# Attention and feed-forward kernel: wide masks built on GpSimd, the first keys and weights loaded from ScalarE's queue, a new launch order, and four buffers for the last tile's stores

## The chip, the cores and the metric

The kernel runs on one NeuronCore of one Trainium2 chip. The metric is the device time of one execution in microseconds (us). Time before: 910.72 us, the median of three runs (909.49 to 911.6).

## The reference

Banded attention over 8 batches, 8 heads, 576 positions and 64 dimensions, and then a feed-forward block on the 4608 tokens of width 512:

```python
scores = scale * np.matmul(q, k.transpose(0, 1, 3, 2))
mask = (rel >= 0) & (rel < 64)                      # rel = query position - key position
scores = np.where(mask, scores, -1000000000.0)
attn = softmax(scores)
x = np.matmul(attn, v)                              # heads joined: 4608 x 512, float32
h = x @ w_in                                        # 512 -> 2048, float64 weights
g = np.where(h >= 1, h, np.where(h <= -1, 0.0, (h + 1) ** 2 / 4))
out = (g @ w_out).astype(np.float32)                # 2048 -> 512
```

## The kernel before

The tokens are cut into 9 tiles of 512 tokens. **Attention** goes in 36 steps of 128 tokens (two blocks of 64), four steps for a tile. A step s loads queries (`load_q`), keys (`load_k`) and two blocks of values (`load_v`); makes scores on TensorE in two halves h, the even and the odd heads (`att_scores`); takes the maximum on VectorE (`att_max`), the exponential on ScalarE (`att_exp`, four heads, eight records), the inverse of the sum and the product with it on VectorE (`att_inverse`, `att_normalize`), turns the result over (on TensorE with a copy out for the first seven steps, `att_transpose_pe` and `att_transposed`; on VectorE later), multiplies with the values (`att_values`), and splits the product into a high and a low part (`att_high`, `att_low`), the tiles `xh` and `xl`. For the first four steps the mask is added by TensorE, as a matmul of an identity `idr` with a rounded mask `mskr`; for the next three VectorE adds a wide mask of 128 columns; later steps use a narrow one of 96 columns.

**Weights** come as float64, one chunk f for 128 of the 2048 hidden units, unit 0 for `w_in` and unit 1 for `w_out` (512 KB each; from chunk 4 on both units in one load of 1 MB). ScalarE and VectorE convert the bits to a high and a low float part, in nine rows: `w_rest` and `w_sign` (ScalarE, out `u` and `raw`), two `w_limit` rows and `w_shift` (VectorE), `w_join` (VectorE), `w_high` (ScalarE), `w_low` (VectorE). **The feed-forward part** of tile t goes over the 16 chunks: `ffn_in` (12 matmuls into `ps_h`), the activation on ScalarE, VectorE and (from tile 1 on) GpSimd, and `ffn_out` (matmuls into `acc`). After the last chunk `ffn_take` copies `acc` into a tile `o` (two buffers) and `ffn_store` sends it out.

The order on each engine is not written by hand. Every piece of work is given to `Plan.add` with a key, a cost per engine, what it needs and what buffers it takes. `Plan.run` places the pieces by these numbers, and each engine's queue holds them in that order and runs them strictly one after the other. All loads and stores are issued from SyncE's queue (SP). At most eight transfers are under way before the next issue waits for an old one to land.

The masks, wide and narrow, come from memory by `load_masks` as the first transfer; `round_masks` then makes `idr` and `mskr` on ScalarE.

Of the kernel before, what the change touches and what calls it, by code (L numbers as in the profile page):

```python
# [44 lines left out]
W_LATE = 2.92
W_LOAD = 1580
V_LATE = 2.54
W0_KEY = -101.5
M_LATE = -3.29
W0_STEP = 2.63  # L50
FINE = 4
NWARM = 8
A_FIRST = (-100.64, -97.76, -95.51, -95)
A_NEXT = 3.31
A_STEP = 4.3
A_SPAN = 9
A_LEAD = 5
O_LAG = 2.5
DMA_LAG = 2300
BEGIN = dict(PE=1500, ACT=2300, DVE=2500, SP=750)  # L60
# [8 lines left out]
B_PE = 2050  # L69
B_DUE = 1.0, 2.5, 0.5  # L70
B_STEP = 16 / 3
B_FIRST = 3.5
A_END = 1.5
V_PE = 1270
NORM = dict(Pool=800, DVE=560), dict(DVE=690)
# [4 lines left out]
class Plan:  # L80
# [82 lines left out]
def banded_attention_then_ffn(ctx: ExitStack, tc: tile.TileContext, q, k, v, w, masks, out, dims):  # L163
# [25 lines left out]

    idt = const.tile([P, P], F32, name="idt")  # L190
    make_identity(nc, idt)
    msk = const.tile([P, 3, 2 * WIN], F32, name="msk")
    idr = const.tile([P, P], F32R, name="idr")
    mskr = const.tile([P, 3, WIN], F32R, name="mskr")
    wpool = ctx.enter_context(tc.tile_pool(name="wpool", bufs=1))

    ptd = [const.tile([P, NP, SB], F32, name=f"ptd{i}") for i in range(BUFS["ptd"])]
    for t in ptd:
# [118 lines left out]
    def variant(s):  # L317
        firsts = [(2 * s + i) % NB == 0 for i in range(2)]
        return 1 if firsts[0] else 2 if firsts[1] else 0

    def near(s):
        return s >= PE_STEPS

    def load_q(s):
        qts[s] = t = ld.tile([P, NP, SB], F32, name="qt", bufs=BUFS["qt"])
        nc.sync.dma_start(out=t, in_=q[s])

    def load_k(s):
# [34 lines left out]

    def att_masked(s, h):
        ps, sm, _, _ = blk[s, h]
        at, n = (WIN, NEAR) if near(s) else (0, WIN)
        m = msk[:, variant(s), at:at + n].unsqueeze(1).broadcast_to([P, NP, n])
# [73 lines left out]
    def add_step(t, i):  # L441

        s = starts[t] // SB + i
        masked = s < PE_MASKS
        joined = SOON <= s < NT // SB - 1
        pt, pv = ("ps_h", "acc") if s < LENT else ("ps_a", "ps_a")
        ps = "acc" if s < FIRST and s % 2 else "ps_a"
        if s < FIRST:
            key = due = A_FIRST[s]
        elif s >= SOON:  # L450
            key = a_keys[s]
        else:
            key = a_keys[s]
            due = min(key + A_SPAN, soon(s))
        lk = key - L_LEAD
        if s == 0:
            last["m"] = add(lk + M_LATE, dict(SP=590), lambda e: load_masks(), lag=DMA_LAG)
            last["r"] = add(lk + M_LATE, dict(ACT=480), lambda e: round_masks(), [last["m"]])
        xq = add(lk, dict(SP=790), lambda e: load_q(s), takes=["qt"], lag=DMA_LAG)
        xk = add(lk, dict(SP=1180), lambda e: load_k(s), takes=["kt"], lag=DMA_LAG)  # L460
        xv = add(lk + V_LATE, dict(SP=790), lambda e: load_v(s, 0), last["v"], takes=["vt"], lag=DMA_LAG)
        xw = add(lk + V_LATE, dict(SP=790), lambda e: load_v(s, 1), [xv], takes=["vt"], lag=DMA_LAG)
        last["v"] = [xw]
        needs = [xq, xk] + [last["r"]] * masked + last["s"]
        if s - 1 in before:
            needs_v, gives_v, split = before.pop(s - 1)

            def do(e):
                att_scores(s, masked, ps)
                att_values(s - 1, "ps_h")  # L470

            xs = add(
                key, dict(PE=B_PE), do, needs + needs_v, takes=[ps, ps, "sm", "sm", "ps_h"],
                gives=[("qt", xq), ("kt", xk)] + gives_v,
            )
            split(xs, key, "ps_h")
        else:
            xs = add(
                key, dict(PE=S_PE[near(s)] + 500 * masked), lambda e: att_scores(s, masked, ps), needs,
                takes=[ps, ps, "sm", "sm"], gives=[("qt", xq), ("kt", xk)],  # L480
            )
        last["s"] = [xs]
        ready, first, taken = [], last["t"], []
        for h in range(2):
            x = xs
            if s >= SOON:
                due = key + B_DUE[0] + B_DUE[2] * h
            if not masked:
                x = add(due, dict(DVE=MASKED[near(s)]), lambda e, h=h: att_masked(s, h), [x, last["m"]], gives=[(ps, xs, h)])
            x = add(due, dict(DVE=950 if masked else MAXIMUM[near(s)]), lambda e, h=h: att_max(s, h, masked), [x])  # L490
            x = add(
                due, dict(ACT=1750 if masked else EXP[near(s)]), lambda e, h=h: att_exp(s, h, masked), [x],
                gives=[(ps, xs, h)] * masked,
            )
# [24 lines left out]
        gives = [("ptd", taken[0]), ("ptd", taken[1]), ("vt", xv), ("vt", xw)]  # L519

        def split(xo, due, pv):
            after = [xo] if i == 0 else [xo, x_first[t]]
            x = add(due, XHIGH, lambda e: att_high(t, i, e), after, takes=["x"] if i == 0 else [])
            if i == 0:
                x_first[t] = x
            x = add(due, dict(DVE=660), lambda e: att_low(t, i), [x], gives=[(pv, xo)])
            x_ready.setdefault(t, []).append(x)

        if joined:
            before[s] = needs, gives, split  # L530
# [58 lines left out]

    os = {}  # L590

    def ffn_take(t, i, eng):
# [31 lines left out]
    def add_ffn(t):  # L624
        first, before, x_out = {}, [x_in[t - 1]] if t else [], {}
        for f in range(NF):
            for r, key in parts(t, f):
# [29 lines left out]
                for k, i in enumerate(subs(r)):  # L657
                    x_out[i] = xo
                    first.setdefault(i, (xo, k))
        for i in range(TILES[t] // P):  # L660
            xo = add(
                key, dict(DVE=690, ACT=590), lambda e, i=i: ffn_take(t, i, e), [x_out[i]], takes=["o"],
                gives=[("acc", *first[i])],
            )
            add(key, dict(SP=790), lambda e, i=i: ffn_store(t, i), [xo], lag=DMA_LAG, gives=[("o", xo)])


    a_keys, key = {}, float("inf")
# [77 lines left out]
```

## Time and profile before

| what | value |
|---|---|
| median of three runs | 910.72 us |
| the profiled execution | 909.63 us, of which its span from first to last instruction is 907.6 us |
| TensorE (PE) busy | 885.1 us, 98% of the span |
| VectorE (DVE) busy | 567.1 us, 62% |
| ScalarE (ACT) busy | 453.9 us, 50% |
| GpSimd (POOL) busy | 168.6 us, 19% |
| mean granted TensorE clock | 0.995 |

Busy time is the time in which an engine had an instruction running; for PE the ends are modelled, so a busy PE is not always at its peak. The shares are means over stages that differ: the first 55 us, in which nothing can be multiplied before it is loaded and converted, the long stretch after that, and the last 5 us.

### The profile page before, as it was taken

Reading aid. Unit: us, or ns where it says so; the run is one execution under the profiler, and the core shown is the slowest. Engines: PE = TensorE matmul, PEld = TensorE weight load, DVE = VectorE, ACT = ScalarE, POOL = GpSimd, SP = SyncE. Lnnn points to the kernel's source line nnn. Section 1 sums busy time; section 2 is a strip of 40 time slices with the busy share of each in tenths; the row PEclk is TensorE's granted clock in tenths of the full one; section 3 lists DMA queues with packets and bytes.
Section 4 is the critical chain, followed back from the end, with each engine's and each line's share of the span. In section 5 each row is a group of like instructions: output and inputs, shape, how many; then the busy total and the mean of one; then the engine's idle time right before and its main releaser. Section 6 shows DMA issues by size and latency. Waiting matters only on the chain.

```text
span 907.6 us, 17441 instructions
## 1 busy us (share of the span) xinstructions
PE 885.1 (98%) x6888; PEld 729.6 (80%) x6888; DVE 567.1 (62%) x1406; ACT 453.9 (50%) x1148; POOL 168.6 (19%) x142
## 2 busy tenths in 40 slices
PE   6789999999999999999999999999999999999997
PEld 5678788888888888888888888888888888888886
DVE  5999987778766666666666666667666766622111
ACT  6898965544544445444544443445444444433333
POOL 0000001212222221222122222122212221222221
PEclk8999999999999999999999999999999999999999
DMA  8982023111221122111211121112111220001001
GB/s 314 380 353 70 21 85 115 55 60 53 77 76 54 53 77 76 53 54 53 100 53 54 48 77 43 42 51 99 53 54 53 77 76 25 12 1 47 1 0 47
DMA packets 29281, 70.14 MB, mean 77 GB/s; under 512 B 3216, under 2 KB 3600, under 8 KB 29200
## 3 DMA queue, kind: packets, MB, share of 16 engines
q1 hardware_dynamic: 29200, 69.03, 21.8%
q8 instruction: 54, 0.88, 0.4%
q14 instruction: 27, 0.22, 0.1%
HBM read 59.58 MB, written 9.44 MB: 76 GB/s over the span
## 4 chain that ended last, share of the span: by engine, by line
PE 89%; DVE 6%; ACT 2%; issue 1%; DMA 1%; SPq 0%; ACTq 0%; DVEq 0%
PE acc L585 41%; PE ps_h L544 40%; PE ps_h L420 3%; PE ps_a L356 3%; DVE u L271 1%; ACT wts L215 1%; DVE raw L248 1%; DVE wts L283 1%; DMA raw<-in_w 1%; PE ps_a L420 1%; DVE gl L576 1%; DVE raw L260 1%; DVE sm L391 1%; PE ps_a L406 0%; ACT u L267 0%
## 5 line engine op out<-in xcount | busy, mean ns | idle before, releaser
L544 PE MATMUL ps_h<-xh,wts 128*128 128x512 f32 (+1 forms) x1232 | 382.5, 376 | 3.5 <-DVE a L566 2.9
L585 PE MATMUL acc<-wts,gh 128*128 128x512 f32 x1152 | 360.2, 394 | 0.0
L576 POOL TENSOR_TENSOR gl<-a,gh 128x512 fp32r<-128x512 f32 (+1 forms) x135 | 167.1, 1238 | 730.4 <-ACT gh L571 724.8
L544 PEld LDWEIGHTS ps_h<-xh,wts 128*128 128x128 f32 x1232 | 227.0, 188 | 47.2 <-DVE a L566 3.5
L566 DVE SCALAR_TENSOR_TENSOR a<-a,ps_h 128x512 f32<-128x512 f32 (+1 forms) x154 | 100.2, 652 | 256.0 <-ACT a L559 240.4
L585 PEld LDWEIGHTS acc<-wts,gh 128*128 128x128 f32 x1152 | 212.9, 188 | 45.0 <-issue 0.3
L544 PE MATMUL ps_h<-xl,wts 128*128 128x512 f32 (+1 forms) x616 | 231.4, 376 | 0.6 <-DVE xl L433 0.6
L585 PE MATMUL acc<-wts,gl 128*128 128x512 f32 x576 | 224.3, 389 | 0.0
L554 ACT ACTIVATE a<-ps_h 128x512 f32<-128x512 f32 (+1 forms) x154 | 87.8, 570 | 262.4 <-PE ps_h L544 260.5
L400 DVE STREAM_TRANSPOSE ptd<-sm 32x128 f32<-32x128 f32 x696 | 210.7, 303 | 10.9
L571 ACT CAST gh<-a 128x512 fp32r<-128x512 f32 (+1 forms) x154 | 91.0, 592 | 102.5 <-DVE a L566 88.6
L544 PEld LDWEIGHTS ps_h<-xl,wts 128*128 128x128 f32 x616 | 115.9, 188 | 21.8 <-DVE xl L433 0.8
L585 PEld LDWEIGHTS acc<-wts,gl 128*128 128x128 f32 x576 | 108.1, 188 | 23.5 <-DVE gl L576 0.2
L379 ACT ACTIVATE sm<-sm,nm 128x96 f32<-128x96 f32 (+1 forms) x256 | 93.1, 365 | 42.3 <-DVE nm L372 42.2
L559 ACT ACTIVATE a<-a 128x512 f32<-128x512 f32 (+1 forms) x150 | 91.2, 608 | 4.7
L379 ACT ACTIVATION_READ_ACCUMULATOR sm<-sm,nm 128x1 f32 x256 | 48.0, 188 | 0.0
L368 DVE SCALAR_TENSOR_TENSOR sm<-ps_a,msk 128x384 f32<-128x384 f32 (+1 forms) x64 | 35.9, 562 | 13.9 <-PE ps_a L356 13.9
L391 DVE TENSOR_TENSOR sm<-sm,den 128x384 f32<-128x384 f32 (+1 forms) x71 | 41.5, 584 | 2.3
L356 PEld LDWEIGHTS ps_a<-kt,qt 64*32 64x32 f32 (+1 forms) x2016 | 27.4, 108 | 14.1 <-issue 13.4
L372 DVE TENSOR_REDUCE nm<-sm 128x4 f32<-128x384 f32 (+1 forms) x64 | 36.1, 563 | 1.7
L356 PE MATMUL ps_a<-kt,qt 64*32 64x96 f32 (+1 forms) x2016 | 34.8, 251 | 1.7 <-DMA kt<-in_k 1.7
L420 PE MATMUL ps_h<-ptd,vt 128*64 128x64 f32 x864 | 31.1, 225 | 0.0
(59 smaller groups left out, 350.1 us busy)
## 6 DMA issues: line engine op xcount, KB each, us to landing
vt<-in_v SPq DMA_DIRECT2D x72, 256.0 KB, 3.5
kt<-in_k SPq DMA_DIRECT2D x36, 384.0 KB, 4.5
raw<-in_w SPq DMA_DIRECT2D x12, 1023.8 KB, 11.5
qt<-in_q SPq DMA_DIRECT2D x36, 256.0 KB, 3.7
out<-o SPq DMA_DIRECT2D x36, 256.0 KB, 2.0
raw<-in_w SPq DMA_DIRECT2D x8, 511.8 KB, 7.0
msk<-in_masks SPq DMA_DIRECT2D x1, 336.0 KB, 3.6
```

The source lines that it names most:

```text
L356: nc.tensor.matmul(banks[h][r, p, :n], lhsT=qt[half[h], p, r], rhs=kt[half[h], p, i * m:i * m + n], start=not masked, stop=not masked or p ...
L379: nc.scalar.activation(sm[:, p, :], (ps if masked else sm)[:, p, :], AF.Exp, bias=nm[:, p:p + 1], scale=scale if masked else 1.0, accum_ou ...
L391: engine[eng].tensor_tensor(out=sm, in0=sm, in1=den.unsqueeze(2).broadcast_to(sm.shape), op=ALU.mult)
L400: nc.vector.transpose(pt[(c + j) * SQ:(c + j + 1) * SQ, :, r], sm[r, :, c * SQ:(c + 1) * SQ])
L420: nc.tensor.matmul(ps[half[h], p, n], lhsT=vt[i][:, c:c + D], rhs=pt[h][:, p, n], start=True, stop=True)
L544: nc.tensor.matmul(ps, lhsT=wts[f, 0][:, part, c * P:(c + 1) * P], rhs=x[:, c, r], start=(c == 0 and j == 0), stop=(c == NP - 1 and j == 2),)
L554: nc.scalar.activation(gs[t, f, r.start][0], phs[t, f, r.start], AF.Relu, bias=0.5, scale=0.5)
L559: nc.scalar.activation(a, a, AF.Square)
L566: nc.vector.scalar_tensor_tensor(out=a, in0=a, scalar=1.0, in1=ps, op0=ALU.min, op1=ALU.max)
L571: nc.scalar.copy(g[1], g[0])
L576: engine[eng].tensor_tensor(out=g[2], in0=g[0], in1=g[1].bitcast(F32), op=ALU.subtract)
L585: nc.tensor.matmul(acc[t, i], lhsT=g[:, sub], rhs=wts[f, 1][:, part], start=(f == 0 and j == 0), stop=(f == NF - 1 and j == 2),)
```

## The change

Four things, beside the numbers that the plan works with.

1. `load_masks` no longer stands first. GpSimd makes the wide mask at the start of the program with `memset`, `affine_select` and copies, and only the narrow masks are loaded, into a tile `nmsk`, before step 5's data. `round_masks` needs GpSimd's work instead of a transfer, and rounds two of the three variants.
2. The keys of step 0 and the first 512 KB of weights, chunk 0 unit 0, are issued from ScalarE's queue. All others stay on SP's.
3. The numbers of the plan are changed, and with them the order of rows on every engine in the first two tiles.
4. The last tile's four results go through the four buffers of the attention pool `sm`, and no longer through the two of `o`.

```diff
-W_FIRST = (20.66, 3.1)
+W_FIRST = (20.66, 2.83)
...
+    for n, at in ((P, QB), (QB, 0)):
+        m = msk[:n, 0]
+        nc.gpsimd.memset(m, 0.0)
+        nc.gpsimd.affine_select(
+            out=m, in_=m, compare_op=ALU.is_ge, fill=NEG, base=at - 1, pattern=[[1, WIN]], channel_multiplier=-1
+        )
+        nc.gpsimd.affine_select(
+            out=m, in_=m, compare_op=ALU.is_ge, fill=NEG, base=WINDOW - at, pattern=[[-1, WIN]], channel_multiplier=1
+        )
+    for n, r in ((1, slice(0, QB)), (2, slice(QB, P))):
+        nc.gpsimd.tensor_copy(msk[:, n], msk[:, 0])
+        nc.gpsimd.memset(msk[r, n, :QB], NEG)
...
-        nc.sync.dma_start(out=t[:, :4 * m - 1], in_=src.rearrange("p u n -> p (u n)")[:, 1:])
+        (nc.scalar if g == (0, (0,)) else nc.sync).dma_start(out=t[:, :4 * m - 1], in_=src.rearrange("p u n -> p (u n)")[:, 1:])
...
-        nc.sync.dma_start(out=t, in_=k[s])
+        (nc.scalar if s == 0 else nc.sync).dma_start(out=t, in_=k[s])
...
-        nc.sync.dma_start(out=msk[:, :, :WIN + NEAR], in_=masks)
+        nc.sync.dma_start(out=nmsk[:, :, :NEAR], in_=masks)
...
-        nc.scalar.mul(mskr, msk[:, :, :WIN], 1.0 / scale)
+        nc.scalar.mul(mskr[:, :2], msk[:, :2], 1.0 / scale)
...
-        os[t, i] = o = ffn.tile([P, DM], F32, name="o", bufs=BUFS["o"])
+        if pool == "o":
+            o = ffn.tile([P, DM], F32, name="o", bufs=BUFS["o"])
+        else:
+            o = att.tile([P, NP, WIN], F32, name="sm").rearrange("p a n -> p (a n)")
+        os[t, i] = o
...
+        pool = "sm" if t == len(TILES) - 1 else "o"
```

How rows move, at three places. The lines of the changed kernel are later than those of the kernel before by 19 in this part (L379 there is L398 here).

ScalarE at the start of the program, before. `u` and `raw` are the first two conversions of a weight chunk, `sm,den` the exponentials of step 0.

```order
L341 ACT_TABLE_LOAD
L341 CAST idr<-idt 128x128
L342 ACTIVATE mskr<-msk 128x384
L267 ACTIVATE u<-raw 128x512
L244 ACTIVATE raw<-raw 128x512
L267 ACTIVATE u<-raw 128x512
L379 ACTIVATE sm,den<-ps_a,nm 128x128 x8
```

And in the changed kernel:

```order
L360 ACT_TABLE_LOAD
L360 CAST idr<-idt 128x128
L361 ACTIVATE mskr<-msk 128x256
L349 DMA kt<-in_k 128x768
L253 DMA raw<-in_w 128x2047
L286 ACTIVATE u<-raw 128x512
L263 ACTIVATE raw<-raw 128x512
L286 ACTIVATE u<-raw 128x512
L263 ACTIVATE raw<-raw 128x512
L398 ACTIVATE sm,den<-ps_a,nm 128x128 x8
```

The two issues stand behind the row that makes `mskr`, which waits for GpSimd, and a fourth conversion row stands ahead of the exponentials of step 0.

SyncE's queue at the start, before (`qt`, `kt`, `vt` are queries, keys and values, `raw` weights):

```order
L338 DMA msk<-in_masks 128x3x224
L326 DMA qt<-in_q 128x512
L330 DMA kt<-in_k 128x768
L234 DMA raw<-in_w 128x2047 x2
L335 DMA vt<-in_v 128x512
L326 DMA qt<-in_q 128x512
L330 DMA kt<-in_k 128x768
L234 DMA raw<-in_w 128x2047
```

And in the changed kernel:

```order
L345 DMA qt<-in_q 128x512
L253 DMA raw<-in_w 128x2047
L345 DMA qt<-in_q 128x512
L349 DMA kt<-in_k 128x768
L253 DMA raw<-in_w 128x2047
L354 DMA vt<-in_v 128x512
L253 DMA raw<-in_w 128x2047
```

Step 1's queries and keys stand third and fourth, not seventh and eighth, and the weights that stand second are chunk 0 unit 1.

VectorE and ScalarE where the first steps end. On VectorE in the changed kernel, from the last half of step 3 (`den`, `sm`) to the weights of chunk 1 unit 1 (the last two rows):

```order
L405 TENSOR_SCALAR den<-den 128x4
L406 RECIPROCAL den<-den 128x4
L452 TENSOR_TENSOR xl<-ps_a,xh 128x4x128
L410 TENSOR_TENSOR sm<-sm,den 128x512
L302 TENSOR_TENSOR wts<-u,wts 128x512 x2
L586 SCALAR_TENSOR_TENSOR a<-a,ps_h 128x256
L267 TENSOR_SCALAR raw<-raw 128x512 x2
L279 TENSOR_SCALAR raw<-raw 128x512
```

and on ScalarE in the changed kernel, from the last exponentials of step 3 to the `raw` row that the VectorE rows above need:

```order
L398 ACTIVATE sm,den<-acc,nm 128x128 x4
L234 CAST xh<-ps_a 128x4x128
L234 CAST wts<-u 128x512 x2
L579 ACTIVATE a<-a 128x256
L234 COPY ptd_110<-ps_a 128x512
L286 ACTIVATE u<-raw 128x512 x2
L263 ACTIVATE raw<-raw 128x512
```

On VectorE before, the same weights of chunk 1 unit 1 were worked on ahead of that last half of step 3:

```order
L248 TENSOR_SCALAR raw<-raw 128x512 x2
L260 TENSOR_SCALAR raw<-raw 128x512
L271 TENSOR_TENSOR u<-u,raw 128x512
L561 TENSOR_TENSOR a<-a 128x256
L566 SCALAR_TENSOR_TENSOR a<-a,ps_h 128x256
L386 TENSOR_SCALAR den<-den 128x4
L387 RECIPROCAL den<-den 128x4
L433 TENSOR_TENSOR xl<-ps_a,xh 128x4x128
L391 TENSOR_TENSOR sm<-sm,den 128x512
```

The `wts` rows of chunk 0 unit 1 and chunk 1 unit 0 stand behind the last normalization of step 3 now; before, they stood between steps 1 and 2.

## Rows read from the trace of the kernel before

**Rows 1.** The page: busy us, share of the span and instructions of each engine.

```profile
PE 885.1 (98%) x6888; PEld 729.6 (80%) x6888; DVE 567.1 (62%) x1406; ACT 453.9 (50%) x1148; POOL 168.6 (19%) x142
```

**Rows 2.** Stretches of the span: length, busy us, granted clock, DMA share, GB/s.

```profile
8.40:15.00 6.60, 2.73 (x35) 2.00 (x36) 4.80 (x14) 5.27 (x21) 0.00 (x0) 0.77 1.03 406
15.00:25.00 10.00, 6.80 (x84) 5.38 (x84) 9.55 (x25) 7.57 (x26) 0.00 (x0) 0.81 0.99 364
25.00:40.00 15.00, 11.01 (x168) 9.30 (x168) 13.84 (x37) 14.32 (x50) 0.00 (x0) 1.00 0.97 366
55.00:100.00 45.00, 45.00 (x253) 36.66 (x252) 42.87 (x67) 40.67 (x63) 0.00 (x0) 1.00 0.33 123
```

**Rows 3.** The chain that ended last, in order of time: start, us, what.

```profile
2.55 6.63 DMA raw<-in_w
...
24.10 0.64 PE ps_h L406 x4
24.77 0.59 ACT ptd L215
...
103.90 2.76 PE acc L585 x12
```

**Rows 4.** Timeline, first 30 us: start, us, row, idle time before.

```profile
4.36 0.52 ACT L342 ACTIVATE mskr<-msk 128x384 fp32r<-128x384 f32 x1 [2.03 <-DMA msk<-in_masks]
...
9.21 0.66 ACT L267 ACTIVATE u<-raw 128x512 uint32<-128x512 uint32 x1 [4.33 <-DMA raw<-in_w]
...
9.90 0.65 ACT L244 ACTIVATE raw<-raw 128x512 bf16<-128x512 bf16 x1
...
11.04 0.35 ACT L379 ACTIVATE sm<-ps_a,nm 128x128 f32<-128x128 f32 x1
...
12.56 0.17 DVE L386 TENSOR_SCALAR den<-den 128x4 f32<-128x4 f32 x1 [1.03 <-ACT sm L379]
...
12.92 1.99 PE L356 MATMUL acc<-kt,qt 64*64 64x128 f32 x32 [3.87 <-DMA kt<-in_k]
...
25.46 1.28 DVE L283 TENSOR_TENSOR wts<-u,wts 128x512 fp32r<-128x512 f32 x2
...
29.25 0.38 PE L544 MATMUL ps_h<-xh,wts 128*128 128x256 f32 x1 [0.57 <-ACT xh L215]
```

**Rows 5.** GpSimd's first rows by shape: count, busy us, mean ns, idle before.

```profile
L576 POOL TENSOR_TENSOR gl<-a,gh 128x256 fp32r<-128x256 f32 x6 | 4.4, 734 | 151.0 <-ACT gh L571 151.0
masks.py:199 POOL TENSOR_SCALAR_AFFINE_SELECT idt<-idt 128x128 f32<-128x128 f32 x1 | 0.3, 293 | 0.1
masks.py:197 POOL MEMSET idt<- 128x128 f32 x1 | 0.2, 206 | 0.3 <-POOLq L735 0.3
```

**Rows 6.** Timeline of SyncE's queue: start and us of the issues.

```profile
0.73 0.66 SPq L338 DMA_DIRECT2D msk<-in_masks  x1
1.45 0.58 SPq L326 DMA_DIRECT2D qt<-in_q  x1
2.55 0.91 SPq L234 DMA_DIRECT2D raw<-in_w  x2
```

**Rows 7.** Line L326, first queries: from issue to landing.

```profile
DMA to landing us min/median/max: 3.5/3.5/3.5
```

**Rows 8.** Line L234, the first two weight loads: from issue to landing.

```profile
DMA to landing us min/median/max: 6.6/7.0/7.4
```

**Rows 9.** DVE by shape, first 60 us: count, busy us, mean ns, idle before.

```profile
L391 DVE TENSOR_TENSOR sm<-sm,den 128x512 f32<-128x512 f32 x8 | 5.5, 689 | 0.2
```

**Rows 10.** Timeline of the end: takes and stores of the last tile.

```profile
901.23 0.69 DVE L217 COPY o<-acc 128x512 f32<-128x512 f32 x1 [2.43 <-PE acc L585]
...
902.16 0.39 PE L585 MATMUL acc<-wts,gl 128*128 128x512 f32 x1
903.29 0.59 ACT L215 COPY o<-acc 128x512 f32<-128x512 f32 x1 [2.15 <-DMA out<-o]
904.07 0.59 ACT L215 COPY o<-acc 128x512 f32<-128x512 f32 x1 [0.19 <-DMA out<-o]
```

More of the change, by code (lines that the diff above doesn't have):

```diff
@@ L41 @@
 W_LEAD = 0.57
-W_FIRST = (20.66, 3.1)
+W_FIRST = (20.66, 2.83)
 W_STEP = 4 / 3
 L_LEAD = 2
[L45 to L50, printed above, removed]
+W_LATE = 3.88
+W_LOAD = 1290
+Q_LOAD = 650
+K_LOAD = 980
+V_LATE = 4.31
+W0_KEY = -101.44
+M_LATE = 0
+W0_STEP = 2.32
 FINE = 4
 NWARM = 8
-A_FIRST = (-100.64, -97.76, -95.51, -95)
-A_NEXT = 3.31
-A_STEP = 4.3
+A_FIRST = (-101.37, -97.76, -95.51, -95)
+A_NEXT = 2.99
+A_STEP = 4.44
 A_SPAN = 9
@@ L58 @@
 O_LAG = 2.5
-DMA_LAG = 2300
-BEGIN = dict(PE=1500, ACT=2300, DVE=2500, SP=750)
+O_LAG_DMA = 2300
+DMA_LAG = 1300
+BEGIN = dict(PE=1500, ACT=2300, DVE=2500, SP=2700)
 PERIOD = 10240 / 3
@@ L71 @@
 B_STEP = 16 / 3
-B_FIRST = 3.5
+B_FIRST = 3.44
 A_END = 1.5
@@ L191, in banded_attention_then_ffn @@
     make_identity(nc, idt)
-    msk = const.tile([P, 3, 2 * WIN], F32, name="msk")
+    msk = const.tile([P, 3, WIN], F32, name="msk")
+    nmsk = const.tile([P, 3, WIN], F32, name="nmsk")
     idr = const.tile([P, P], F32R, name="idr")
@@ L365, in att_masked @@
         ps, sm, _, _ = blk[s, h]
-        at, n = (WIN, NEAR) if near(s) else (0, WIN)
-        m = msk[:, variant(s), at:at + n].unsqueeze(1).broadcast_to([P, NP, n])
+        m = nmsk[:, variant(s), :NEAR] if near(s) else msk[:, variant(s)]
+        m = m.unsqueeze(1).broadcast_to(sm.shape)
         nc.vector.scalar_tensor_tensor(out=sm, in0=ps, scalar=scale, in1=m, op0=ALU.mult, op1=ALU.add)
@@ L456, in add_step @@
         if s == 0:
+            last["r"] = add(lk, dict(ACT=480), lambda e: round_masks())
+        if s == PE_STEPS - 2:
             last["m"] = add(lk + M_LATE, dict(SP=590), lambda e: load_masks(), lag=DMA_LAG)
[L458 to L462, printed above, removed]
+        xq = add(lk, dict(SP=Q_LOAD), lambda e: load_q(s), takes=["qt"], lag=DMA_LAG)
+        xk = add(lk, dict(SP=K_LOAD), lambda e: load_k(s), takes=["kt"], lag=DMA_LAG)
+        xv = add(lk + V_LATE, dict(SP=Q_LOAD), lambda e: load_v(s, 0), last["v"], takes=["vt"], lag=DMA_LAG)
+        xw = add(lk + V_LATE, dict(SP=Q_LOAD), lambda e: load_v(s, 1), [xv], takes=["vt"], lag=DMA_LAG)
         last["v"] = [xw]
@@ L488, in add_step @@
             if not masked:
-                x = add(due, dict(DVE=MASKED[near(s)]), lambda e, h=h: att_masked(s, h), [x, last["m"]], gives=[(ps, xs, h)])
-            x = add(due, dict(DVE=950 if masked else MAXIMUM[near(s)]), lambda e, h=h: att_max(s, h, masked), [x])
+                x = add(due, dict(DVE=MASKED[near(s)]), lambda e, h=h: att_masked(s, h), [x, last["m"]] if near(s) else [x], gives=[(ps, xs, h)])
+            x = add(due, dict(DVE=900 if masked else MAXIMUM[near(s)]), lambda e, h=h: att_max(s, h, masked), [x])
             x = add(
-                due, dict(ACT=1750 if masked else EXP[near(s)]), lambda e, h=h: att_exp(s, h, masked), [x],
+                due, dict(ACT=1500 if masked else EXP[near(s)]), lambda e, h=h: att_exp(s, h, masked), [x],
                 gives=[(ps, xs, h)] * masked,
@@ L590, in banded_attention_then_ffn, with ffn_take @@
     os = {}
-    def ffn_take(t, i, eng):
-        os[t, i] = o = ffn.tile([P, DM], F32, name="o", bufs=BUFS["o"])
+    def ffn_take(t, i, eng, pool):
+        if pool == "o":
[3 more added lines that the diff above has]
+        os[t, i] = o
         copy(eng, o, acc[t, i])
@@ L659, in add_ffn @@
                     first.setdefault(i, (xo, k))
+        pool = "sm" if t == len(TILES) - 1 else "o"
         for i in range(TILES[t] // P):
             xo = add(
-                key, dict(DVE=690, ACT=590), lambda e, i=i: ffn_take(t, i, e), [x_out[i]], takes=["o"],
+                key, dict(DVE=690, ACT=590), lambda e, i=i: ffn_take(t, i, e, pool), [x_out[i]], takes=[pool],
                 gives=[("acc", *first[i])],
             )
-            add(key, dict(SP=790), lambda e, i=i: ffn_store(t, i), [xo], lag=DMA_LAG, gives=[("o", xo)])
+            add(key, dict(SP=790), lambda e, i=i: ffn_store(t, i), [xo], lag=O_LAG_DMA, gives=[(pool, xo)])
     a_keys, key = {}, float("inf")
@@ L716 @@
     ).view(np.int64)
-    row = np.arange(P)[:, None] % QB
+    row = np.arange(P)[:, None] % SQ
     block = np.arange(P)[:, None] // QB
-    key = np.arange(WIN)[None, :] - QB
-    seen = (row - key >= 0) & (row - key < WINDOW)
-    wide = [seen & ((key >= 0) | (block != first)) for first in (-1, 0, 1)]
-    row = np.arange(P)[:, None] % SQ
     near = np.arange(NEAR)[None, :] - WINDOW
@@ L729 @@
     seen = (row - near >= 0) & (row - near < WINDOW)
-    narrow = [seen & ((key >= 0) | (block != first)) for first in (-1, 0, 1)]
-    masks = np.concatenate(
-        [np.stack([np.where(m, 0.0, NEG) for m in ms], axis=1) for ms in (wide, narrow)], axis=2
+    masks = np.stack(
+        [np.where(seen & ((key >= 0) | (block != first)), 0.0, NEG) for first in (-1, 0, 1)], axis=1
     ).astype(np.float32)
```

## The prediction

> **What bounds the kernel now.** I began with the busy line of the page: TensorE works for 98% of the span [rows 1], so at first sight only less TensorE work could help, and this change removes none. The stretches say where the other 2% are: between 8.4 and 40 us TensorE is busy for 20.5 of 31.6 us (2.73, 6.80 and 11.01), while VectorE is busy for 9.55 of 10 and 13.84 of 15 us and ScalarE for 14.32 of 15; from 55 us on TensorE is full, 45.00 of 45 [rows 2]. The chain of waits agrees: it begins with the first weights, which land at 2.55 + 6.63 = 9.18 us, and goes through rows of VectorE and ScalarE, with short pieces of TensorE, until 103 us; from 103.90 on it is TensorE alone [rows 3]. So time is to be had in two places: at the start, where the first rows of VectorE and ScalarE begin late and then have no room, and at the end, behind the last matmul. What the change makes earlier or later for VectorE there counts about one for one; what it does to transfers counts only through the first row that waits for them.
>
> The sums go against the profiled execution, 909.63 us (a span of 907.6 and 2.0 around it), and are then put on the median of 910.72, which is 1.1 above it.
>
> **The end.** The last matmul starts at 902.16 and ends at 902.55. The third take waits 2.15 us for a store to give its buffer back, and the fourth comes behind it and ends at 904.07 + 0.59 = 904.66 [rows 10]. With four buffers the last take has only the last matmul before it: in the new order it is a VectorE copy like the one at 901.23, 0.69 us, so it ends at 903.24. That is **-1.4 us**. What follows (one store and its landing) is as before. Nothing hides this gain, since nothing is behind it; its bounds are 1.3 and 1.5 (one copy on either engine), as no other row stands there.
>
> **GpSimd's masks.** GpSimd has no row between the identity and its first `gl`, which waits for ScalarE for 151 us in all before its first six [rows 5], so it has the time. Ahead of `mskr` stand three memsets at 0.21, five selects at 0.29, two copies and two small memsets. The trace has no copy on GpSimd; it lies between a memset (0.21) and the 128x256 `gl` row (0.73), and I take 0.3, as a 128x128 row has half the columns. The sum is 0.62 + 1.47 + 0.6 + 0.3 = 3.0, with 0.1 between dependent rows (the idle time before the select, [rows 5]) about 3.7, from 0.73 on: 4.4 us. With the ends for the copies and no waits 3.5 to 5.3. The old `mskr` started at 4.36, when its transfer had landed [rows 4]. So the masks themselves cost and bring nothing. Their load of 336 KB goes from the front of the queue (0.85 us at the 406 GB/s of 8.4 to 15 us, [rows 2]); the narrow one comes much later, between loads that run far ahead.
>
> **The first keys and weights.** Here the order tells what the diff doesn't: both issues stand on ScalarE behind `mskr`, so they leave at about 4.4 and 4.9 us, where SyncE issued the weights at 2.55 [rows 3]. By then SyncE has issued the first queries, weights unit 1, step 1's queries and keys, and more: 1920 KB besides the queries. When do they land? The first queries landed at 1.45 + 3.5 = 4.95 [rows 6, 7]; without the masks ahead I take 4.1. The weights followed at 9.18: 896 KB (keys and weights) in 4.2 us, where 406 GB/s makes it 2.3, so about 2.0 us were lost just when the first weights began. The trace doesn't say to what; the first weights again follow the first queries, so I let it come again (bounds 0 and 2.0) and have two queues at work from 6.1 us. ScalarE's has 896 KB. Served first, it is through at 8.3; in equal shares at 10.6; in order of issue, behind the 1920 KB, at 13.2. I take **10.3**, close to equal shares. Before it was 9.18 [rows 3, 8].
>
> The Trainium skill, "DMA: Bandwidth & Descriptors", section "Queues, rings and completion order", says that each transfer engine goes round between the queues that have work, packet by packet; by it the sum would be the equal shares, 10.6. All loads went by one queue here, so no row shows two.
>
> ScalarE started its conversions at 9.21 and the exponentials of step 0 at 11.04, three rows later [rows 4]. Now four conversion rows stand ahead of them, at 0.6 more (the starts at 9.90 and 11.04 are two rows apart): 10.3 + 1.86 + 0.6 = 12.8, or **+1.8 us**; by the ends -0.2 and +4.7. VectorE's first `den`, at 12.56 before, follows at 14.3, and behind it wait all other VectorE rows. VectorE has little to put into the gap: only maxima that it had to do anyway.
>
> **The new order.** Up to the last row of chunk 4's weights, VectorE has nearly the same rows ahead in both orders: one row of 128x512 and two of half that size more now, one copy less; up to chunk 6 no more than before. A row of 128x512 takes 0.69 [rows 9], so this is 0 to 0.7; I take **+0.5**.
>
> One wait is new. In the third place shown, VectorE's `raw` rows of chunk 1 unit 1 need ScalarE's `raw` row, which stands behind the copy of step 3's last half, and this needs that half's normalization on VectorE. From the end of the normalization: transposes 0.64, copy 0.59 [rows 3], two `u` rows at 0.57 each, the `raw` row 0.65 [rows 4]: 3.0 us. VectorE has two `wts` rows, 1.28 for two [rows 4], and a gate row of half a 128x512 row's columns, 0.4 (0.69 for a whole one, [rows 9]): 1.7. So it stands for **1.3 us**, and behind it on its queue stand the rest of chunk 1 and all of chunk 2, for which TensorE waits. Before, these rows were done ahead of that half. The bounds are 0 (if ScalarE comes to it early) and 1.7.
>
> For the same reason the weights of chunk 1 unit 0 are ready later: between the first `den` and the last normalization of step 3 stand 16 short `den` rows, 8 normalizations, 6 maxima and some 17 others, about 21 us of work, so TensorE can begin chunk 1 at about 37 us. That is the effect of the terms above, not another one.
>
> Sum: -1.4 + 1.8 + 0.5 + 1.3 = **+2.2 us**: 911.8 for such an execution, **912.9** on the median.
>
> **Rivals.** *ScalarE's queue is served early.* If its two transfers are through at 8.3, the exponentials are at -0.2 and the sum is -1.4 - 0.2 + 0.5 + 1.3 = +0.2: 910.9. For it: SyncE's queue loses its time first, with weights. Against: it issues 2 us later than before.
>
> *Step 1 sets the pace, and the change gains.* TensorE waited 3.87 us for step 1's keys, until 12.92 [rows 4]. They stand fourth in the queue now, behind 512 KB of weights and 256 KB of queries, with 384 KB of their own; in equal shares 896 KB of these 1152 are through at 10.6, the other 256 at 11.2, so steps 1 to 3 could run 1.7 us earlier, and TensorE's first chunk, at 29.25 before [rows 4], too. It decides where VectorE has step 0 done before step 1 needs it: if the 2.1 us that VectorE is idle between 55 and 100 us [rows 2] and this lead take up the late start and the wait, and a third of the lead (0.6) is left, the sum is -1.4 - 0.6 = -2.0: 908.7. Against: the chain goes through VectorE up to 103 us.
>
> *TensorE's clock stays down longer.* The clock was 0.77 and 0.81 in the stretches to 15 and to 25 us [rows 2], that is 1.2 GHz for some 3.0 and 3.8 us, after the idle time of 3.87. Now TensorE has only one step's scores and two transposes in that time, so one more such stretch at 1.2 GHz can follow. It holds scores (1.99 for a step, [rows 4]), transposes (0.64) and values, 2 to 4 us by my estimate from these rows; half of the doubled time is on the path, 1 to 2 us: 914 to 915.
>
> **How the numbers follow.** A measurement of this kernel can tell about 0.2%, 1.8 us: faster is below 908.9, slower above 912.5. Forecast 0.45, its own range 911.8 to 914; early service 0.2; step 1's pace 0.18; the clock 0.17. Of the forecast about two thirds lie above 912.5. So faster 0.18, the same 0.35, slower 0.47. The range leaves out half of the clock's case and a part of the gain: **909.0 to 914.9**.
>
> **What would show it.** Right: both ScalarE issues after 4 us; first `u` row after 9.7; exponentials of step 0 after 12.3; a wait of over 1 us of VectorE's `raw` row for ScalarE near 38 us; chunk 1 on TensorE after 36; the last take on VectorE with no wait for a store. Wrong: weights from ScalarE's queue landing by 8.5, or TensorE full from before 50 us on.

## The result, and the profile after

The changed kernel takes 914.83 us (median of six, 914.62 to 915.75), the kernel before in the same session 910.32 (909.36 to 911.6). The ratio is 1.0049, with an interval of 1.0037 to 1.0062: 4.5 us slower. The profiled execution has 914.64 us, a span of 912.8, against 907.6 before.

The stretches, as in [rows 2]: length, busy us of TensorE, its loads, VectorE, ScalarE and GpSimd, granted clock (1.00 is 2.4 GHz, 0.50 is 1.2 GHz), DMA share, GB/s.

```profile
8.40:15.00 6.60, 4.17 (x54) 3.22 (x58) 2.04 (x6) 1.90 (x3) 0.00 (x0) 0.62 0.72 284
15.00:25.00 10.00, 6.92 (x70) 4.90 (x66) 6.29 (x19) 7.50 (x34) 0.00 (x0) 0.50 0.93 313
25.00:40.00 15.00, 10.65 (x165) 8.72 (x158) 13.75 (x35) 12.72 (x49) 0.00 (x0) 0.93 1.02 399
55.00:100.00 45.00, 43.40 (x248) 34.91 (x248) 42.45 (x69) 41.58 (x68) 0.00 (x0) 1.00 0.33 123
```

From 8.4 to 25 us VectorE works 8.33 us where it worked 14.35, ScalarE 9.40 where it worked 12.84. The clock is 0.50 all through 15 to 25 us, that is 1.2 GHz. TensorE is no longer full between 55 and 100 us. That goes with the new order and not with the late start: one of the runs below, in the new order but with its loads back on SyncE's queue, is faster than the kernel before and has it too, while in the order of before TensorE works all 45.00 us there with early issues as well. The stretch in the run with the loads back on SyncE's queue:

```profile
55.00:100.00 45.00, 43.55 (x245) 34.70 (x244) 42.29 (x66) 39.77 (x64) 0.00 (x0) 1.00 0.25 90
```

The chain that ended last (followed back from the last instruction, at each step to what released it), its first part (start, us, what):

```profile
0.88 0.21 POOL msk L204
...
3.57 0.10 POOL msk L214
3.69 0.39 ACT mskr L361
4.11 8.93 DMA raw<-in_w
13.06 0.68 ACT u L286
...
15.60 2.90 ACT sm L398 x16
...
19.78 1.10 PE ps_h L425 x4
...
21.54 1.97 PE acc L439 x30
...
24.66 1.92 PE ps_a L375 x32
```

It now begins with GpSimd's masks, goes through the row that rounds them to the issue of the first weights, and waits 8.93 us for them, to 13.04; before it was 2.55 + 6.63 = 9.18 [rows 3]. Four transposes on TensorE take 1.10 where they took 0.64 [rows 3].

ScalarE's timeline at the start, with its queue's issues:

```profile
3.69 0.42 ACT L361 ACTIVATE mskr<-msk 128x256 fp32r<-128x256 f32 x1 [1.36 <-POOL msk L214]
3.70 0.38 ACTq L349 DMA_DIRECT2D kt<-in_k  x1
4.11 0.66 ACTq L253 DMA_DIRECT2D raw<-in_w  x1
13.06 0.67 ACT L286 ACTIVATE u<-raw 128x512 uint32<-128x512 uint32 x1 [8.95 <-DMA raw<-in_w]
...
15.60 0.35 ACT L398 ACTIVATE sm<-ps_a,nm 128x128 f32<-128x128 f32 x1
```

The first conversion starts at 13.06 (9.21 in [rows 4]) and the exponentials of step 0 at 15.60 (11.04): 4.56 us later.

SyncE's queue:

```profile
3.59 0.52 SPq L253 DMA_DIRECT2D raw<-in_w  x1
12.89 0.33 SPq L345 DMA_DIRECT2D qt<-in_q  x1
```

and what its queue waited for in the first 16 us (us in total, times, longest):

```profile
SPq L345 <- PE ps_a L375: 7.2, 1, 7.2
```

The queries of step 2 need a buffer that step 0's scores give back, and these wait for the keys on ScalarE's queue. SyncE issues nothing from 4.1 to 12.89 us: first it waits 1.5 us for an earlier load of weights to land, and then 7.2 us for those scores. The DMA view from 12.9 to 13.6 us shows the gap behind it:

```profile
DMA packets 0, 0.00 MB, mean 0 GB/s; under 512 B 0, under 2 KB 0, under 8 KB 0
```

The same view from 8.5 to 10.5 us, by queue (q10 is ScalarE's, q1 SyncE's; packets, MB, share of the 16 engines):

```profile
q10 hardware_dynamic: 161, 0.50, 61.9%
q1 hardware_dynamic: 161, 0.33, 42.8%
```

From 4 to 7.3 us it has SyncE's queue alone:

```profile
q1 hardware_dynamic: 392, 1.02, 89.7%
```

So ScalarE's keys, issued at 3.70, moved nothing until 7.3. The two queues then moved as many packets as each other only in the middle: from 7.3 to 8.5 us ScalarE's had 38 to SyncE's 98, and from 10.5 to 12.5 us

```profile
q1 hardware_dynamic: 120, 0.43, 52.1%
q10 hardware_dynamic: 88, 0.30, 36.7%
```

From 7.3 to 12.5 us ScalarE's queue moved 0.92 MB, which is its 896 KB, and SyncE's 1.10 MB.

VectorE's new wait, at the first `raw` rows of chunk 1 unit 1:

```profile
42.63 0.62 DVE L267 TENSOR_SCALAR raw<-raw 128x512 int16<-128x512 int16 x2 [1.58 <-ACT raw L263]
```

And the end, the last matmul and the last take:

```profile
908.63 0.39 PE L605 MATMUL acc<-wts,gl 128*128 128x512 f32 x1
```

```profile
909.06 0.69 DVE L236 COPY sm<-acc 128x512 f32<-128x512 f32 x1 [0.67 <-PE acc L605]
```

The take follows the matmul and no store: 909.75 - 908.63 = 1.12 us from the start of the last matmul to the end of the last take, against 904.66 - 902.16 = 2.50 [rows 10].

### The profile page after: what moved, and what is told of

The parts are those of the page before. It is cut to its first block, busy times and chain, and to the rows that moved or that the text cites. A ratio compares the mean times of both kernels' runs of the same rounds, so it can differ in the third digit from the quotient of the medians.

```text
span 912.8 us, 17459 instructions
## 1 busy us (share of the span) xinstructions
PE 892.5 (98%) x6888; PEld 733.4 (80%) x6888; DVE 567.9 (62%) x1407; ACT 452.4 (50%) x1148; POOL 169.4 (19%) x151
## 4 chain that ended last, share of the span: by engine, by line
PE 86%; DVE 7%; ACT 4%; issue 2%; DMA 1%; POOL 0%; ACTq 0%; POOLq 0%; DVEq 0%
PE acc L605 40%; PE ps_h L564 39%; PE ps_h L439 3%; PE ps_a L375 3%; DVE u L290 2%; DVE raw L267 1%; DVE wts L302 1%; DMA raw<-in_w 1%; ACT u L286 1%; ACT wts L234 1%; ACT sm L398 1%; DVE raw L279 1%; PE ps_a L439 0%; ACT raw L263 0%; DVE sm L410 0%
## 5 line engine op out<-in xcount | busy, mean ns | idle before, releaser
L398 ACT ACTIVATE sm<-sm,nm 128x96 f32<-128x96 f32 (+1 forms) x256 | 93.0, 365 | 40.9 <-DVE nm L391 40.9
L398 ACT ACTIVATION_READ_ACCUMULATOR sm<-sm,nm 128x1 f32 x256 | 47.9, 187 | 0.0
L387 DVE SCALAR_TENSOR_TENSOR sm<-ps_a,nmsk 128x384 f32<-128x384 f32 x58 | 31.9, 550 | 13.8 <-PE ps_a L375 13.8
```

Source lines behind the costliest of these rows:

```text
L398: nc.scalar.activation(sm[:, p, :], (ps if masked else sm)[:, p, :], AF.Exp, bias=nm[:, p:p + 1], scale=scale if masked else 1.0, accum_ou ...
```

## The experiments

The theories. **A:** the loss is the late landing from ScalarE's queue, far beyond the predicted 1.1 us. **B:** the new order loses by itself. **C:** the clock, 1.2 GHz up to 27 us, is a part of its own. In every run the keys and the weights were moved together, so what each of the two cost is not told apart. Ratios are to the kernel before, run beside each; 0.001 is 0.9 us. The order of rows on each engine is exactly that of the kernel named, but for the edit.

**The four buffers alone**, in the kernel before:

```diff
-        os[t, i] = o = ffn.tile([P, DM], F32, name="o", bufs=BUFS["o"])
+        if pool == "o":
+            o = ffn.tile([P, DM], F32, name="o", bufs=BUFS["o"])
+        else:
+            o = att.tile([P, NP, WIN], F32, name="sm").rearrange("p a n -> p (a n)")
+        os[t, i] = o
...
+        pool = "sm" if t == len(TILES) - 1 else "o"
```

> The kernel before with one edit: the last tile's four results go through the four buffers of the attention pool. Order of all other rows as before. Theory of the prediction: the takes no longer wait 2.15 us for a store, the last one is a copy of 0.69 us right behind the last matmul (902.55), so 1.4 us less: ratio 0.9985, 909.0 us against 910.4. Rival: the wait only moves to the last store, and nothing is gained: 910.4.

Measured 0.9989 (0.9980 to 0.9998), 1.0 us less; the predicted 1.4 is inside. The gain is real and the store did not take it back.

**The masks alone**, in the kernel before:

```diff
     def load_masks():
-        nc.sync.dma_start(out=msk[:, :, :WIN + NEAR], in_=masks)
+        pass
...
+        if s == PE_STEPS - 2:
+            nc.sync.dma_start(out=nmsk[:, :, :NEAR], in_=masks)
```

(with GpSimd's rows of the change).

> The kernel before, in exactly its order, with the wide masks made by GpSimd and only the narrow ones loaded, much later; the tail as before. If the masks are ready in time and cost nothing (the row that rounds them ended at about 4.1 us in the changed kernel), the first queries, keys and weights move up by the 336 KB that no longer stand ahead of them, 0.8 us: weights at 8.4 and not 9.18, exponentials of step 0 at 10.2 and not 11.04, and the time is 0.4 to 0.8 us less, 909.6 to 910.0. Rival (the start is not the bound, or the weights meet the same loss of 2 us at another place): no difference. Rival (GpSimd's masks are what costs in the changed kernel): 1 us or more slower.

Measured 0.9980 (0.9970 to 0.9990), 1.8 us less, more than expected. ScalarE's timeline:

```profile
7.18 0.66 ACT L282 ACTIVATE u<-raw 128x512 uint32<-128x512 uint32 x1 [3.06 <-DMA raw<-in_w]
...
9.19 0.35 ACT L396 ACTIVATE sm<-ps_a,nm 128x128 f32<-128x128 f32 x1
```

The weights are there 2.0 us before [rows 4], not 0.8. By themselves GpSimd's masks cost nothing; in the changed kernel they count only because ScalarE's issues stand behind them.

**The loads back on SyncE's queue**, in the changed kernel:

```diff
-        (nc.scalar if g == (0, (0,)) else nc.sync).dma_start(out=t[:, :4 * m - 1], ...
+        nc.sync.dma_start(out=t[:, :4 * m - 1], ...
-        (nc.scalar if s == 0 else nc.sync).dma_start(out=t, in_=k[s])
+        nc.sync.dma_start(out=t, in_=k[s])
```

> The changed kernel, in exactly its order, but with the keys of step 0 and the first weights issued by SyncE's queue again, where its order puts them (queries, keys, weights unit 0, weights unit 1). Theory A, the late landing from ScalarE's queue is the larger part of the loss: the keys land at about 6.5 and not 10.7, the weights at about 8.5 and not 13.0, the exponentials of step 0 start at about 11.0 and not 15.6, SyncE's queue no longer stands still from 4 to 12.9 us for the scores of step 0, and the time falls from 914.8 to 910 (909 to 911). Theory B, the new order loses by itself (the 1.58 us that VectorE waits for ScalarE near 41 us, and rows ahead of others): it stays at 912.5 or more.

Measured 0.9989 (0.9979 to 0.9998): 5.5 us of 1.0049 are gone, and the kernel is faster than before. ScalarE's timeline:

```profile
7.36 0.66 ACT L286 ACTIVATE u<-raw 128x512 uint32<-128x512 uint32 x1 [3.24 <-DMA raw<-in_w]
...
9.93 0.35 ACT L398 ACTIVATE sm<-ps_a,nm 128x128 f32<-128x128 f32 x1
```

The exponentials start 5.67 us before those of the changed kernel. Theory A holds, and B, as the larger part, falls. What followed from the late landing went with it: SyncE's long stop, and a part of the low clock (0.79 from 15 to 25 us, for 0.50). The new order is not free, though; the chain of this run goes through loads of values that it issues later:

```profile
17.64 7.70 DMA vt<-in_v
```

**ScalarE's issues at the head of its queue**, in the changed kernel:

```diff
     with tc.manual_schedule():
+        load_k(0)
+        w_load((0, (0,)))
         plan.run()
```

(and not where the plan had them).

> The changed kernel, in exactly its order, but with ScalarE's two issues at the head of its queue, ahead of the identity and the row that waits for GpSimd. It tells why that queue delivered late. If because its issues stood behind the masks: they leave at about 0.8 and 1.3 us, both queues share evenly, and 896 KB of each are through at 1.5 + 4.4 + the 2 us lost at the start, about 8 us; time 909.5 to 911. If because a transfer from this queue begins 3.7 us after its issue (issue 3.70, first packet 7.4 in the changed kernel) wherever it stands: first packet at 4.5, weights at about 10.0 us, time 911 to 912.5. Theory B, the new order loses by itself: 912.5 or more in any case.

Measured 0.9975 (0.9964 to 0.9985), 6.7 us better than the change.

```profile
0.74 0.41 ACTq L349 DMA_DIRECT2D kt<-in_k  x1
...
7.82 0.66 ACT L286 ACTIVATE u<-raw 128x512 uint32<-128x512 uint32 x1 [3.70 <-DMA raw<-in_w]
...
10.37 0.34 ACT L398 ACTIVATE sm<-ps_a,nm 128x128 f32<-128x128 f32 x1
```

The same queue, 3 us earlier, has the weights there at 7.8. It is not slow; it was late, behind the masks. Against SyncE's queue alone (7.36, ratio 0.9989) the second queue brought the weights no earlier, and the intervals of the two runs overlap.

**Masks and four buffers together**, in the order of before, all loads on SyncE's queue (the two edits above):

> The kernel before, in exactly its order, with GpSimd's masks and with the four buffers for the last tile; all loads on SyncE's queue. Beside the changed kernel with its loads back on SyncE's queue (ratio 0.9989 to before) it tells what the new order costs or brings. The two parts alone gave 0.9989 and 0.9980; if they add up, this gives 0.9969, 907.5 us where before is 910.3. If the new order costs 1.8 us, as the prediction's two terms for it say (0.5 and 1.3), this is 1.8 us faster than the new order with the same loads. Rival: the order is worth nothing either way, and this gives 0.9989 too, because the gains of the start and of the end don't add up.

Measured 0.9979 (0.9968 to 0.9990), 1.9 us less, not the sum of 2.8, though that is inside. Beside 0.9989 the new order costs 0.9 us, with an uncertainty of about 1.4: not settled by this pair. In its profile the weights came late:

```profile
9.32 0.66 ACT L282 ACTIVATE u<-raw 128x512 uint32<-128x512 uint32 x1 [5.21 <-DMA raw<-in_w]
```

with the loads and the order with which they were there at 7.18. But the profiled execution took 910.65 us, the slowest of its twelve (median 908.31), so this late landing need not be that of the others.

**The same, with early issues from ScalarE** (the edit of the early run, in the order of before):

> The kernel before, in exactly its order, with GpSimd's masks, four buffers for the last tile, and the first keys and weights issued at the head of ScalarE's queue. In the new order the early issue from ScalarE gave 0.9975 and the same loads on SyncE's queue 0.9989; if that is worth the same here, this gives 0.9955. If the two queues only share the same transfers (the weights landed at 7.8 and at 7.3 us in the new order), it gives 0.9969, as without ScalarE's queue.

Measured 0.9966 (0.9955 to 0.9977), 3.1 us less. ScalarE's timeline:

```profile
7.88 0.66 ACT L282 ACTIVATE u<-raw 128x512 uint32<-128x512 uint32 x1 [3.77 <-DMA raw<-in_w]
...
9.69 0.35 ACT L396 ACTIVATE sm<-ps_a,nm 128x128 f32<-128x128 f32 x1
```

**The same, with late issues**, all of the change but its order:

```diff
     with tc.manual_schedule():
+        round_masks()
         load_k(0)
         w_load((0, (0,)))
         plan.run()
```

> As the run before this one, but with ScalarE's two issues behind the row that waits for GpSimd's masks, as in the changed kernel: all of the change but its order. Theory A (the late issue is the larger part of the loss, in whatever order): keys at about 10.5, weights at about 13 us, the exponentials of step 0 near 15, and 4 to 5.5 us slower than with early issues: ratio 1.000 to 1.003. Theory B' (late landing only hurts in an order that wants the weights early): 0.997 to 0.999.

Measured 1.0024 (1.0012 to 1.0036): 5.3 us slower than with early issues, so A holds in this order too.

```profile
3.69 0.38 ACTq L347 DMA_DIRECT2D kt<-in_k  x1
...
12.91 0.68 ACT L282 ACTIVATE u<-raw 128x512 uint32<-128x512 uint32 x1 [8.81 <-DMA raw<-in_w]
...
14.76 0.35 ACT L396 ACTIVATE sm<-ps_a,nm 128x128 f32<-128x128 f32 x1
```

Three pairs now differ by the order alone: 0.9989 and 0.9979, 0.9975 and 0.9966, 1.0049 and 1.0024. The new order is slower by 0.9, 0.8 and 2.3 us, all of one sign. The first two are within their noise (about 1.4 us each); the third is not (about 1.6), but a second run of the change, further down, gave 1.0032, and beside that it is 0.7. The third pair also differs in the clock: from 8.4 to 15 and from 15 to 25 us it was 1.00 and 0.66 in the order of before, 0.62 and 0.50 in the new one.

**More idle work on TensorE at the start**, in the changed kernel:

```diff
-        x = add(-200, dict(PE=218 * NWARM), lambda e: warm(NWARM), takes=["acc"])
+        x = add(-200, dict(PE=218 * NWARM), lambda e: warm(NWARM + 10), takes=["acc"])
```

> The changed kernel, in exactly its order, with 18 instead of 8 of TensorE's idle multiplications at the start, which write no result; they take 0.47 us each and fill TensorE until about 10 us, where it was idle from 5.5 to 10.8. The clock was at 1.2 GHz from about 10.8 to 27 us. If that low clock is part of the loss, TensorE is at 2.4 GHz for the scores of steps 0 and 1, and for the transposes and values behind them if the next idle time of 2.5 us leaves it up; the transposes take 0.64 and not 1.08 us, the values 1.0 and not 2.0, and the time is 1 to 2 us less, ratio 1.0030 to 1.0040. If it is hidden behind VectorE and ScalarE: no difference, 1.0049.

Measured 1.0038 (1.0024 to 1.0051), 1.0 us better in the middle, but the intervals overlap. TensorE's timeline:

```profile
1.46 6.31 PE L224 MATMUL acc<-ptd 128*128 128x128 f32 x36 [1.46 <-DVE ptd L218]
...
11.26 1.10 PE L375 MATMUL ps_a<-kt,qt 64*64 64x128 f32 x32 [3.01 <-DMA kt<-in_k]
...
18.82 1.08 PE L425 MATMUL ps_h<-idt,sm 128*128 128x128 f32 x4 [3.61 <-DVE sm L410]
```

All 18 ended at 1.46 + 6.31 = 7.77, not near 10 (0.35 us each and not 0.47), so TensorE was idle again for 3.01 us before the keys. Step 0's scores ran at 2.4 GHz (1.10 for 1.99), but the next idle time of 3.61 left the transposes at 1.2 GHz (1.08). So the run did not lift the clock where the chain went through it, and C is not told apart from nothing.

**SyncE held back until ScalarE has issued**, in the changed kernel:

```diff
+        if s == 1:
...
+            nc.gpsimd.memset(t[:, 0, :1], 0.0)
+            nc.sync.dma_start(out=t, in_=q[s])
+            return
```

> The changed kernel, in exactly its order, but SyncE's second load of queries has to wait for a short GpSimd row behind the masks (it clears a corner of the buffer that the load fills). So ScalarE's two issues at 3.7 us find only 768 KB of SyncE's ahead of them (first queries and one weight load), not 2688 KB. It asks why the first packet of ScalarE's queue came 3.7 us after its issue in the changed kernel, where it came 1.8 us after in the run with early issues. If a late queue's transfer stands behind what the other queue had already issued: first packet about 1.5 us after the issue, keys at about 8 and weights at about 10 us, although half of the loads now leave later; the time falls by 2 to 3 us, to 1.002. If the delay of 3.7 us belongs to an issue in the middle of the start, whatever is ahead: first packet at 7.4, weights at 11 to 12 us, and 1.004 or more.

Measured 1.0032 (1.0021 to 1.0043), and it tells nothing on its question, because the edit did not do what it was for. GpSimd ran the row among the masks' rows:

```profile
1.60 0.10 POOL L346 MEMSET qt<- 128x1 f32 x1
```

```profile
1.73 0.35 SPq L347 DMA_DIRECT2D qt<-in_q  x1
```

SyncE's issue left at 1.73 (1.65 in the changed kernel). This is in effect a second run of the change: 2.9 us slower than before where the first was 4.5. The two intervals meet, so the size of the loss is known to about a microsecond and a half.

**Three buffers for queries**, in the changed kernel:

```diff
-        qts[s] = t = ld.tile([P, NP, SB], F32, name="qt", bufs=BUFS["qt"])
+        qts[s] = t = ld.tile([P, NP, SB], F32, name="qt", bufs=3)
```

> The changed kernel, in exactly its order, with three buffers for queries and not two. In it SyncE's queue stood still from 4.0 to 12.9 us: its next load, the queries of step 2, waited for the scores of step 0, which waited for the keys from ScalarE's queue; no packet moved from 12.9 to 13.6 us. If that stop is a part of the loss: the loads behind it come 2 to 4 us earlier, and the time falls by 0.5 to 1.5 us (1.0035 to 1.0045). If it is not (the rows that wait for those loads are late anyway, or the loads only take room from ScalarE's): 1.0049 or a little above.

Measured 1.0039 (1.0025 to 1.0052), not told from 1.0049. SyncE's waits:

```profile
SPq L349 <- DMA kt<-in_k: 3.8, 1, 3.8
SPq L349 <- PE ps_a L375: 2.1, 1, 2.1
```

The stop moved one step on, to the keys of step 2 (L349), which need a buffer of step 0's scores too. The profiled execution is the slowest of its seven (918.65 us, median 915.16), so its other rows are not set beside those of the change. What the stop costs by itself stays open.

**The new wait taken away**, in the changed kernel with early issues; the order on ScalarE:

```diff
-COPY ptd<-ps_a 128x512
-ACTIVATE u<-raw 128x512 x2
+ACTIVATE u<-raw 128x512
 ACTIVATE raw<-raw 128x512
+COPY ptd<-ps_a 128x512
+ACTIVATE u<-raw 128x512
```

> The changed kernel with early issues from ScalarE (0.9975), with one place of its order changed: on ScalarE the two conversion rows of chunk 1 unit 1 stand ahead of the copy of step 3's last half, and one row of chunk 2 behind it. The prediction's term for the new wait was 1.3 us; in the run with early issues VectorE waited 2.05 us there. If VectorE's wait sets the pace of what follows, it shrinks to about 0.5 and the time falls by 1 to 1.5 us: 0.9959 to 0.9964. If it only moves to the next row: 0.9975.

The wait was, in the early run,

```profile
37.39 0.62 DVE L267 TENSOR_SCALAR raw<-raw 128x512 int16<-128x512 int16 x2 [2.05 <-ACT raw L263]
```

and is now

```profile
35.89 0.62 DVE L269 TENSOR_SCALAR raw<-raw 128x512 int16<-128x512 int16 x2 [0.51 <-ACT raw L265]
...
38.11 0.42 DVE L591 TENSOR_TENSOR a<-a 128x256 f32<-128x256 f32 x1 [0.17 <-ACT a L584]
...
39.77 0.69 DVE L460 TENSOR_TENSOR xl<-ps_a,xh 128x512 fp32r<-128x512 f32 x1 [0.47 <-ACT xh L236]
```

Measured 0.9971 (0.9958 to 0.9984) against 0.9975: of 1.54 us taken from the wait, 0.4 us shows, with an uncertainty of about 1.5, so neither the full price nor none is excluded. Two rows behind it wait now that did not (0.17 and 0.47 us), and the second of them starts only 0.71 us earlier (39.77 for 40.48) where the `raw` rows start 1.50 earlier.

**The fastest version with more idle work on TensorE**: masks, four buffers, early issues, the order of before, and

```diff
-        x = add(-200, dict(PE=218 * NWARM), lambda e: warm(NWARM), takes=["acc"])
+        x = add(-200, dict(PE=218 * NWARM), lambda e: warm(NWARM + 4), takes=["acc"])
```

> The fastest version so far (order of before, GpSimd's masks, four buffers at the end, first keys and weights issued at the head of ScalarE's queue; 0.9966), with 12 instead of 8 of TensorE's idle multiplications at the start, so that it is not idle from 5.5 us until the first keys at 7.4. The clock in that run was 0.65 from 8.4 to 15 us. If the low clock there is on the path: 0.5 us less, 0.9960. If not: 0.9966.

Measured 0.9960 (0.9946 to 0.9974), 3.6 us less than before; not told from 0.9966. The clock in 8.4 to 15 us did rise, from 0.65 in the run without it to 0.96:

```profile
8.40:15.00 6.60, 3.51 (x59) 2.51 (x51) 5.88 (x17) 5.69 (x22) 0.00 (x0) 0.96 1.04 403
```

## Why the prediction was right, and where its sizes were off

The direction and the mechanism held: slower, by a late start above all, less a gain at the end. The range (909.0 to 914.9) held by 0.07 us, and that was luck: the forecast's own range, 911.8 to 914, did not hold, the likeliest time, 912.9, was 1.9 us low, and 914.83 lies where the prediction had put its rival on the clock (914 to 915), which no run showed to be the cause. By its terms:

**The end, -1.4.** Measured alone -1.0 (0.2 to 1.8), and the last take is a VectorE copy with no wait for a store, as predicted.

**GpSimd's masks.** Three memsets, five selects, two copies (0.52 for both) and two small memsets end at 3.86, and the row that rounds the masks starts at 3.69; predicted 4.4, with 3.5 to 5.3. They cost nothing on GpSimd, but they head the chain, since the issues stand behind them. That the loads behind the old mask load come 0.85 us earlier was too little in one run (2.0) and too much in another (0.0: 9.32 for 9.21); what decides between the two is open. The second stands in the slowest execution of its run, the first in one near the median.

**The late start, +1.8.** This is the term that was mis-sized: it measured 4.56 (exponentials at 15.60 for 11.04), close to its upper bound of 4.7. The step that failed is "I take 10.3, close to equal shares" for the landing of the first weights; they landed at 13.04, near the 13.2 that the prediction had for service in order of issue. That nearness is chance, for the loads were not served in order of issue: when ScalarE's queue began, SyncE's had moved 1.64 MB (0.62 before 4 us, 1.02 after) of the 2.75 MB that it had issued by 4.1 us, and the two went on side by side. What stood behind 13.04, counted from the 10.6 of equal shares: ScalarE's queue moved nothing until 7.3 us, where the sum let it start at 6.1 (1.2 us); its 0.92 MB then took until 12.5, where equal shares at 406 GB/s make 4.5 us (0.7 more); and the row that waited was released at 13.04 (0.5 more). SyncE had also issued one more load of 512 KB than the 1920 KB of the sum, so it had enough left to share with ScalarE's queue to the end. The price of this term, with all that followed from it (SyncE's stop and what the late keys did to the clock), is shown by undoing it: 5.5 us with the loads on SyncE's queue, 6.7 with early issues, and 5.3 between early and late issues in the old order, for 5.1 to 5.7 us of earlier exponentials (9.93, 10.37 and 9.69 for 15.60, 15.60 and 14.76). The masks alone fit too: 1.8 us for 1.85 (9.19 for 11.04). So "counts about one for one" held for the start, as far as medians with about 1.4 us of noise can tell.

The Trainium skill, "DMA: Bandwidth & Descriptors", section "Queues, rings and completion order", has the transfer engines go round between queues packet by packet. The 161 to 161 of this trace from 8.5 to 10.5 us agree; the counts before and after that stretch (38 to 98, 88 to 120) are not equal. When the second queue begins, and so a part of the wait until 13 us, is nothing that the rule speaks of. Its section "Issuing engines are not separate DMA queues" says that a second issuing engine saves only the time to initiate a transfer. The runs agree as far as they go: 7.36 us with one queue, 7.82 with two.

**The new order, +0.5, and the new wait, +1.3.** Together 1.8; the three pairs measured 0.9, 0.8 and 2.3, so the sum is of the right size as far as the noise tells. Its split is not shown. The wait is there (1.58 us, and at 42.63 and not near 38, since all before it is late), but taking 1.54 of 2.05 us away brought 0.4 in the medians, with an uncertainty of about 1.5. "For which TensorE waits" counted a wait of VectorE as lost in full; on VectorE itself, of 1.50 us that its rows started earlier, 0.71 were left two waits further on, and what of that reaches the end of the kernel is not shown. Late loads of values, which a run with the new order shows on its chain, were not in the sum at all.

**The sum.** -1.0 for the end, +4.6 for the start and +0.9 for the order is +4.5, the measured difference. That it fits to a tenth is luck, with 0.8 to 2.3 for the order and 2.9 for the second run of the change. The two profiles say the same more loosely: the last matmul starts 6.47 us later (908.63 for 902.16), of which the start is 4.56, and 1.9 are left for the order and all else.

**The rivals.** Early service did not come about, since the issues left late; where they left early it did, with 7.8 us for the predicted 8.3. Step 1 could not set the pace: TensorE takes step 0's scores first, and these waited for the late keys. The clock did stay down, at 1.2 GHz through 15 to 25 us, on rows of the chain: the transposes at 1.10 for 0.64 and the scores of step 2 at 1.92 where a step at 2.4 GHz took 1.10. Ahead of these rows TensorE had been idle, for 4.73 us before the late keys alone; no run took the low clock away by itself, so what part of the 4.5 us it carries is argued and not shown.

What was named to show it right mostly came in: first `u` row after 9.7 (13.06), exponentials after 12.3 (15.60), a wait of over 1 us of the `raw` row (at 42.63, not near 38), chunk 1 on TensorE after 36 (its first row at 40.04), no wait for a store at the end. One did not: the issues stood at 3.70 and 4.11, not both after 4.

## What to carry to other kernels

A transfer moved to another engine's queue is issued when that engine comes to it: read what stands ahead of it there, and ahead of that, before counting bytes. Here the first weights waited behind masks with which they had nothing to do, and the same issue at the head of the same queue turned 4.5 us lost into 2.3 gained. And a load that takes a buffer can stop its whole queue: one late transfer, through the buffer that its reader holds, kept SyncE from issuing for 7.2 us. Last, a profile shows one execution: where it was the slowest of its run, its rows say little about the median.

## What was not expected of the hardware

ScalarE's first transfer began at least 3.6 us after its issue (3.70 to 7.3), with SyncE's queue at work, and 1.8 us after it where both queues had just begun (0.74 to 2.5, the early run). In all four profiles with late issues (the change, SyncE held back, three buffers, and the old order) its first packets lie between 7.3 and 7.6 us. In the early run the DMA view shows its first packets from 2.5 to 2.7 us:

```profile
q10 hardware_dynamic: 8, 0.02, 30.2%
q1 hardware_dynamic: 7, 0.01, 18.4%
```

It did not stand behind all that the other queue had issued, which had moved 1.64 of its 2.75 MB by then; whether it stood behind a part of it is open, since the run that was to tell did not hold SyncE back. Sharing by packets is not sharing by bytes: 161 packets each carried 0.50 and 0.33 MB from 8.5 to 10.5 us. And the landing of the first weights on SyncE's queue, with the same loads in the same order, differed between two profiles by 2.1 us (7.18 in an execution near its run's median, 9.32 in the slowest of its run), while in the runs with early issues from ScalarE it was 7.82 and 7.88.
